# A fused attention and two mixture layers on one core: expert 0's scalings placed later, routing steps reordered, SP in program order

## The chip, the cores and the metric

The kernel runs on one core of a Trainium2 chip. Five engines run side by side, each from its own in-order queue: TensorE (PE, matmuls, with PEld for its weight loads), VectorE (DVE), ScalarE (ACT), GpSimd (POOL) and SyncE (SP, which here issues transfers). SBUF is the on-chip memory; PSUM has 8 banks that matmuls write. The metric is the device time of one execution in microseconds (us); lower is better.

## The reference, cut to what matters

```
x   = attention(q, k, v)         # 2 x 8 heads, 576 tokens, head 64; masks: 4 heads local, 4 strided -> x [1152, 512]
P   = sinkhorn(exp(x @ w_gate))  # 8 rounds over rows and columns, [1152, 8]
x2  = sum over e of P[:, e] * (relu(x @ w1[e]) @ w2[e])            # 8 experts, 512 -> 1024 -> 512, all tokens
nl  = x2 @ wgate2 + log1p(exp(x2 @ wnoise)) * noise
top = two largest of nl per token; w = softmax over the two
out[t] = sum over its two experts e of w * (relu(x2[t] @ v1[e]) @ v2[e])
```

Everything is float32. A matmul of full precision is made of three passes over operands split into a high and a low part (`mm3`).

## The kernel before, in words

Tokens lie in 9 tiles of 128. The first mixture is dense. Expert 0 comes first, in four quarters of its hidden width, summed unscaled into `acc[:, t]`, because P isn't known yet: the Sinkhorn rounds run on DVE meanwhile. Then line 610 multiplies the nine tiles of `acc` by P[:, 0] on ACT, and experts 1 to 6 follow, each in four quarters q. A quarter computes the hidden layer with the seven products p1 to p7 of a Strassen-Winograd scheme, in two halves of the tokens (`Unit`; `keep` on line 643 copies a product out of its bank as `s1` or `s5`, and p6 may write over the bank only then), and then nine `pair2` calls that DVE adds into `acc`, scaled by P (line 561). Weights are fetched by SP into two raw buffers (line 132; 110 in the later stages) and split by ACT and DVE (lines 103 and 105). All this is outside any hand-written order: a planner, which simulates the program with costs of its own, picks for each engine among the instructions that are ready the one that stands earliest in the program, unless it was given a higher priority.

Expert 7 of the first mixture (`g1`: up, `g2`: down, by tiles), the routing of the second mixture, and its expert 0 stand in a block with a hand-written order (`tc.manual_schedule(engines=ORDERED)`, line 893): there the engines named in ORDERED (PE, DVE, ACT) keep the program's order among the block's instructions; POOL and SP are left to the planner, which may also move work from behind the block between them. The list `between` holds steps that `mm3` calls one by one after each matmul, so that small steps are interleaved with large matmuls.

Routing works on three tiles at a time: r0 (tiles 0 to 2), r3 (3 to 5), r6 (6 to 8). `turn(i)` writes a finished tile to the DRAM table `x2d`, transposes it (line 377) and copies it (line 379). `steps` multiplies it by the gate weights (`lp`, line 387; `lg2`, line 396). `choose` finds the two largest (ACT for exp and log, DVE for the rest; the choice is `m`, line 431), `weigh` makes the weights, `place` ranks the tokens of each expert with small matmuls (`rank`, lines 449 to 453) and lets POOL write six blocks of list entries to the DRAM `table` by indirect DMA (line 474). For r6, `sort`, `assemble` and `collect` build the last tokens of expert 0 on chip with one-hot matrices `hot`. `gather` loads a list (SP, line 531) and pulls the rows of its tokens (POOL, line 536); `prep` transposes them (line 722) and splits them.

Expert 0 of the second mixture runs with its up layer (`up`) and its `Down` parts: part (j, h) is token tile j with half h of the hidden width, and POOL adds its result into `out` by indirect DMA (line 795). `rank` orders the other seven experts by load; SP reads their order into registers (line 869), with which the fetches of their weights are addressed. `look` loads their lists. The seven experts follow (`expert`), each with 256 tokens and a rest of 88 to 32 (CAPS - 256); rests up to 64 take `Down.tail`, unsplit matmuls whose output is cut into m pieces across partitions (lines 809 and 813). For the last expert PE keeps program order. A loop behind it, for overfull experts, isn't entered here.

PSUM banks are handed out in turn per tag, two each for a, b, c and d. Routing and `prep` use b; `g1` uses d; `g2` uses a and c.

Of the kernel before, what the change touches and what calls it, by code (L numbers as in the profile page):

```python
# [9 lines left out]
F32 = mybir.dt.float32  # L10
# [4 lines left out]
AF = mybir.ActivationFunctionType  # L15
# [6 lines left out]
NT = N // 128  # L22
# [39 lines left out]
def tile_kernel(ctx: ExitStack, tc: tile.TileContext, qL, kL, vL, qS, kS, vS, wg, u12, w1, w2, wgn, noise, v1, v2, cst, dummy, out):  # L62
# [304 lines left out]
    class Route:  # L367
# [14 lines left out]
        def steps(self):  # L382
            def product(i):
                if i == 0:
                    self.lp = ps("b", "lp")
# [7 lines left out]
            def total(i):  # L393
                if i == 0:
                    self.lg = ps("b", "lg2")
                nc.tensor.matmul(self.lg[:, i * 2 * E:(i + 1) * 2 * E], self.parts[:, i], fold2, start=True, stop=True)
# [212 lines left out]
    for t in range(NT):  # L609
        nc.scalar.activation(acc[:, t], acc[:, t], AF.Copy, scale=P[:, t, 0:1])  # L610

# [67 lines left out]
    for e in range(1, E - 1):  # L679
        for q in range(NP):  # L680
            raw = fetch_u(e, q)
            a, b = conv_wino(raw[0]), conv_u2(raw[1])
            for u in range(2):
# [10 lines left out]
                for_later = [x.p4, x.p3]  # L694
            y = [partial(pair2, b, t, e) for t in (0, 1, 5, 4, 2, 3, 6, 7, 8)]
# [77 lines left out]
    class Down:  # L773
# [28 lines left out]
        def tail(self, raws, hr, tt, k):  # L802
# [9 lines left out]
            for j in range(m):  # L812
                nc.scalar.activation(y[:k, j * d:(j + 1) * d], p[j * w:j * w + k, :d], AF.Copy,
                                     scale=tt[:k, 1:2].bitcast(F32))
# [36 lines left out]
    def rank():  # L851
# [17 lines left out]
        _, values = nc.values_load_multi_w_load_instructions(ordi[:1, :], engines=(mybir.EngineType.SP,), min_val=1, max_val=E - 1)  # L869
        order.extend(values)  # L870
        return past, key, spot
# [20 lines left out]
    ORDERED = {mybir.EngineType.PE, mybir.EngineType.DVE, mybir.EngineType.Activation}  # L892
    with tc.manual_schedule(engines=ORDERED):
# [26 lines left out]
        g2(*b1, (5,), e, False)  # L920
        r0.choose()
        r3.turn(1)
        g1(*a0, whole[2:], 0, (0,))
        r0.weigh()
        r3.turn(2)
        spread(r3, 0, 2, 6, 9, 10, 11)
        r0.place(EARLY, float(LATE))
        g1(*a0, whole[2:], 0, (1,))
# [17 lines left out]
        vs = [conv_w(raws[0])]  # L946
        g2(*b1, (7,), e, False)
        r6.turn(0)
        g2(*b1, (8,), e, False)
        r6.turn(1)  # L950
        prep([x for _, x in got], [128] * len(got), 0)
# [12 lines left out]
        ranked = rank()  # L964
        raws = [fetch_w(weights(v1, order[0], h)) for h in range(2)]
        look()
# [3 lines left out]
        d0 = Down(vs, [t for t, _ in got], [128] * len(got), 0)  # L970
        r6.assemble()
        d0.part(0, 0)
# [5 lines left out]
        rows.product(0)  # L978
        d0.part(1, 1)
        rows.turn(0)  # L980
        rows.product(1)
        ws = [conv_w(raws[0])]
# [6 lines left out]
    def expert(i, ws, got):  # L989
# [19 lines left out]
        d.part(1, 0)  # L1009
        d.tail(raws, tail, tts[2], k)  # L1010
# [105 lines left out]
```

## Time and profile before

| what | value |
|---|---|
| median of 3 runs | 1129.57 us (1128.79 to 1131.33) |
| the profiled execution, its own time | 1126.98 us |
| its span, first to last instruction | 1125.0 us |
| mean granted TensorE clock, share of full | 0.994 |
| PE busy | 1095.7 us, 97% of the span |
| DVE, ACT, POOL busy | 664.7, 393.7, 185.2 us (59%, 35%, 16%) |
| DMA | 98.71 MB, mean 88 GB/s |

Times inside the profile count from the start of the span. Attention and expert 0 of the first mixture fill the first 170 us, experts 1 to 6 go to about 735 us, the hand-ordered block from there to about 900 us, and the seven routed experts to the end. A share of busy time is a mean over these stages; waits are read where they stand.

### The profile page before, as it was taken

The numbers are of one execution on the slowest core, as the hardware profiler recorded it, in microseconds if no ns is written. First come the engines' busy times: TensorE is split into PE (matmuls) and PEld (weight loads), VectorE is DVE, ScalarE is ACT, GpSimd is POOL, SyncE is SP. The second block draws the span as 40 slices with busy tenths as digits, with TensorE's granted clock in tenths as the row PEclk, the third lists the DMA queues.
The fourth block names the chain that finished last, engine by engine and source line by source line (L and its number), as shares of the span: only waits on it lengthen the run. The fifth ranks groups of instructions, "written<-read, shape, count | busy, mean of one in ns | idle before, by whom it ended". The sixth has DMA issues, their size and how long they took to land.

```text
span 1125.0 us, 16986 instructions
## 1 busy us (share of the span) xinstructions
PE 1095.7 (97%) x6683; PEld 959.7 (85%) x6683; DVE 664.7 (59%) x1362; ACT 393.7 (35%) x884; POOL 185.2 (16%) x221
## 2 busy tenths in 40 slices
PE   7999999999999999999999999999998999999996
PEld 6787988999898998899988999899787788888885
DVE  5876795676666766666666666643356364544440
ACT  5631334333322333223332233221133263544441
POOL 3410132111111111211111110000041411222211
PEclk9999999999999999999999999999999999999998
DMA  9711152111111111111111111021122782555541
GB/s 304 217 52 73 38 174 86 38 63 50 38 39 38 55 59 38 38 38 51 64 38 39 38 46 68 4 109 38 57 48 76 175 318 27 195 194 194 171 100 23
DMA packets 31071, 98.71 MB, mean 88 GB/s; under 512 B 6506, under 2 KB 14954, under 8 KB 22412
## 3 DMA queue, kind: packets, MB, share of 16 engines
q1 hardware_dynamic: 16028, 80.52, 20.7%
q0 software_dynamic: 5200, 10.17, 4.5%
q10 hardware_dynamic: 9760, 6.89, 2.0%
q8 instruction: 54, 0.88, 0.3%
q14 instruction: 29, 0.24, 0.1%
HBM read 86.06 MB, written 11.60 MB: 87 GB/s over the span
## 4 chain that ended last, share of the span: by engine, by line
PE 88%; DVE 5%; DMA 3%; ACT 2%; issue 1%; SPq 0%; POOL 0%; POOLq 0%; DVEq 0%; ACTq 0%
PE y L163 42%; PE h L163 16%; PE a L637 13%; PE b L637 7%; PE d L637 3%; PE y L809 2%; DMA raw<-in_u 1%; PE xgt L722 1%; DMA qs<-in_qS 1%; DVE wl L105 1%; DMA wg_sb<-in_wg 1%; DVE u1l L105 1%; DVE acc L565 0%; PE ot L240 0%; ACT acc L610 0%
## 5 line engine op out<-in xcount | busy, mean ns | idle before, releaser
L561 DVE SCALAR_TENSOR_TENSOR acc<-y,P,acc 128x512 f32<-128x512 f32 x216 | 159.4, 748 | 147.0 <-PE y L163 147.0
L163 PE MATMUL y<-u2h,gh 128*128 128x512 f32 x504 | 198.5, 394 | 0.4 <-DVE acc L561 0.4
L163 PE MATMUL y<-u2l,gh 128*128 128x512 f32 x504 | 197.5, 392 | 0.0
L163 PE MATMUL y<-u2h,gl 128*128 128x512 f32 x504 | 189.8, 392 | 0.4 <-DVE gl L101 0.3
L153 POOL TENSOR_TENSOR ut<-raw 128x256 f32<-128x256 f32 x48 | 35.0, 751 | 509.8 <-DVE u1l L105 430.0
L163 PEld LDWEIGHTS y<-u2h,gl 128*128 128x128 f32 x504 | 94.4, 188 | 20.9 <-DVE gl L101 1.7
L163 PE MATMUL h<-xl,wh 128*128 128x384 f32 (+8 forms) x352 | 110.8, 315 | 0.0
L163 PE MATMUL h<-xh,wh 128*128 128x384 f32 (+8 forms) x352 | 109.9, 315 | 0.6 <-ACT xh L103 0.3
L163 PE MATMUL h<-xh,wl 128*128 128x384 f32 (+8 forms) x352 | 110.1, 313 | 0.0
L163 PEld LDWEIGHTS y<-u2h,gh 128*128 128x128 f32 x504 | 94.8, 188 | 15.8 <-issue 0.8
L163 PEld LDWEIGHTS y<-u2l,gh 128*128 128x128 f32 x504 | 94.8, 188 | 14.2
L100 ACT ACTIVATE hh<-h 128x256 fp32r<-128x256 f32 (+2 forms) x88 | 35.8, 415 | 99.8 <-PE h L163 96.0
L163 PEld LDWEIGHTS h<-xh,wh 128*128 128x128 f32 x352 | 66.5, 190 | 2.0 <-DVE hl L101 0.6
L163 PEld LDWEIGHTS h<-xl,wh 128*128 128x128 f32 x352 | 66.6, 189 | 1.5 <-issue 1.0
L103 ACT ACTIVATE u2h<-raw 128x1024 fp32r<-128x1024 f32 x31 | 32.9, 1061 | 98.9 <-PE y L163 98.9
L163 PEld LDWEIGHTS h<-xh,wl 128*128 128x128 f32 x352 | 66.6, 189 | 0.3 <-issue 0.2
L101 DVE SCALAR_TENSOR_TENSOR hl<-h,hh 128x256 fp32r<-128x256 f32 (+2 forms) x88 | 40.5, 464 | 38.8 <-ACT hh L100 37.0
L637 PE MATMUL a<-sh,u1h 128*128 128x288 f32 x192 | 57.4, 299 | 2.7 <-ACT s L643 2.7
L105 DVE TENSOR_TENSOR wl<-raw,wh 128x1024 fp32r<-128x1024 f32 x42 | 49.5, 1221 | 17.6 <-ACT wh L103 17.6
L637 PE MATMUL a<-sh,u1l 128*128 128x288 f32 x192 | 57.3, 298 | 0.0
L637 PE MATMUL a<-sl,u1h 128*128 128x288 f32 x192 | 57.1, 298 | 0.0
L637 PE MATMUL b<-sh,u1h 128*128 128x288 f32 x192 | 56.7, 295 | 0.0
(245 smaller groups left out, 2497.7 us busy)
## 6 DMA issues: line engine op xcount, KB each, us to landing
raw<-in_u SPq DMA_DIRECT2D x31, 1024.0 KB, 4.7
raw<-in_v SPq DMA_DIRECT2D x20, 1024.0 KB, 8.9
acc<-in_v SPq DMA_DIRECT2D x12, 1024.0 KB
raw<-in_w SPq DMA_DIRECT2D x4, 1024.0 KB
out<-zero ACTq DMA_DIRECT2D x1, 3072.0 KB
x2d<-acc ACTq DMA_DIRECT2D x9, 256.0 KB, 2.0
vs<-in_vL SPq DMA_DIRECT2D x4, 432.0 KB, 10.1
acc<-in_qL SPq DMA_DIRECT2D x3, 576.0 KB
```

The source lines that it names most:

```text
L100: seen[0] = nc.scalar.activation(hi, src, AF.Relu)
L101: nc.vector.scalar_tensor_tensor(lo, src, 0.0, hi.bitcast(F32), op0=ALU.max, op1=ALU.subtract)
L103: seen[0] = nc.scalar.activation(hi, src, AF.Copy)
L105: nc.vector.tensor_tensor(lo, src, hi.bitcast(F32), op=ALU.subtract)
L153: nc.gpsimd.tensor_tensor(t[:, o], x, y, op=ALU.subtract)
L163: nc.tensor.matmul(o, a, b, start=start, stop=stop)
L561: nc.vector.scalar_tensor_tensor(acc[:, t], p, P[:, t, scale:scale + 1], acc[:, t], op0=ALU.mult, op1=ALU.add)
L637: nc.tensor.matmul(p, l[:, b, c], m, start=first and i == 0, stop=i == 5, skip_group_check=not first)
L722: nc.tensor.transpose(p[:, o:o + k], xg[:k, c * 128:(c + 1) * 128], ident[:k, :k])
L809: nc.tensor.matmul(p[j * w:j * w + k, :d], hr[:, f, :k], raws[f // 4][:, f % 4, j * d:(j + 1) * d], start=f == 0, stop=f == 7)
```

## The change

Seven edits. (1) The nine scalings of line 610 now stand in the program behind the fourteen products of expert 1's first quarter. (2) `lp` takes a bank of tag a and `lg2` one of tag c. (3) r3's turns 1 and 2 move ahead of r0's choose and weigh; r0's place moves behind the next quarter of g1. (4) SP joins ORDERED. The four steps of expert 0's `prep` are spread over g2's tile 8, one after every third matmul; the conversion of v2's first half moves behind tile 8. (5) `rank` no longer loads the registers; `names` loads one before the fetch of the first expert's v1 and six behind it. (6) Part (0, 0) moves ahead of `assemble`; the conversion of the first ordered v1 half moves ahead of part (1, 1). (7) In the last expert, the tail comes behind all four parts; in every tail, odd pieces are read by DVE.

```diff
@@ -382,7 +382,7 @@
         def steps(self):
             def product(i):
                 if i == 0:
-                    self.lp = ps("b", "lp")
+                    self.lp = ps("a", "lp")
                 for c in range(NC):
                     nc.tensor.matmul(self.lp[32 * c:32 * c + 32, i * 128:(i + 1) * 128], wgn_sb[:, c], self.xt[i][:, c],
                                      start=True, stop=True)
@@ -392,7 +392,7 @@
 
             def total(i):
                 if i == 0:
-                    self.lg = ps("b", "lg2")
+                    self.lg = ps("c", "lg2")
                 nc.tensor.matmul(self.lg[:, i * 2 * E:(i + 1) * 2 * E], self.parts[:, i], fold2, start=True, stop=True)
 
             return [partial(product, i) for i in range(RB)] + [partial(total, i) for i in range(RB)]
@@ -606,9 +606,6 @@
         marks.append(seen[0].ins)
     with tc.issue_after(marks[1]):
         sums()
-    for t in range(NT):
-        nc.scalar.activation(acc[:, t], acc[:, t], AF.Copy, scale=P[:, t, 0:1])
-
     with tc.issue_after(seen[0].ins):
         nc.scalar.dma_start(wgn_sb, wgn)
         nc.scalar.dma_start(noise_sb, noise)
@@ -692,6 +689,9 @@
                 x.p2()
                 x.p7()
                 for_later = [x.p4, x.p3]
+            if e == 1 and q == 0:
+                for t in range(NT):
+                    nc.scalar.activation(acc[:, t], acc[:, t], AF.Copy, scale=P[:, t, 0:1])
             y = [partial(pair2, b, t, e) for t in (0, 1, 5, 4, 2, 3, 6, 7, 8)]
             y[0]()
             x.p4()
@@ -810,8 +810,11 @@
                                      start=f == 0, stop=f == 7)
             y = gpool.tile([128, DM], F32, tag="y", name="y", bufs=3)
             for j in range(m):
-                nc.scalar.activation(y[:k, j * d:(j + 1) * d], p[j * w:j * w + k, :d], AF.Copy,
-                                     scale=tt[:k, 1:2].bitcast(F32))
+                o, r, f = y[:k, j * d:(j + 1) * d], p[j * w:j * w + k, :d], tt[:k, 1:2].bitcast(F32)
+                if j % 2:
+                    nc.vector.tensor_scalar(o, r, f, None, op0=ALU.mult)
+                else:
+                    nc.scalar.activation(o, r, AF.Copy, scale=f)
             self.send(y, tt, k)
 
     def down(ws, tts, ns, o, last=False):
@@ -866,9 +869,11 @@
         nc.vector.tensor_tensor(big, spot, iota8[:, None, 1:].to_broadcast([128, n, n]), op=ALU.mult)
         nc.vector.tensor_reduce(at, big, axis=AX.X, op=ALU.add)
         nc.vector.tensor_copy(ordi, at)
-        _, values = nc.values_load_multi_w_load_instructions(ordi[:1, :], engines=(mybir.EngineType.SP,), min_val=1, max_val=E - 1)
+        return past, key, spot
+
+    def names(i, j):
+        _, values = nc.values_load_multi_w_load_instructions(ordi[:1, i:j], engines=(mybir.EngineType.SP,), min_val=1, max_val=E - 1)
         order.extend(values)
-        return past, key, spot
 
     def limits(past, key, spot):
         n = E - 1
@@ -889,7 +894,7 @@
     bigi = cpool.tile([1, 1], I32, name="bigi")
 
     raws = fetch_w(w1[0, 1]), fetch_w(w2[0, 1])
-    ORDERED = {mybir.EngineType.PE, mybir.EngineType.DVE, mybir.EngineType.Activation}
+    ORDERED = {mybir.EngineType.PE, mybir.EngineType.DVE, mybir.EngineType.Activation, mybir.EngineType.SP}
     with tc.manual_schedule(engines=ORDERED):
         g1(*a0, whole[:2], 0, (0, 1, 2))
         a1 = conv_w(raws[0])
@@ -918,14 +923,14 @@
         g2(*b1, (4,), e, False)
         r3.turn(0)
         g2(*b1, (5,), e, False)
+        r3.turn(1)
         r0.choose()
-        r3.turn(1)
         g1(*a0, whole[2:], 0, (0,))
+        r3.turn(2)
         r0.weigh()
-        r3.turn(2)
         spread(r3, 0, 2, 6, 9, 10, 11)
+        g1(*a0, whole[2:], 0, (1,))
         r0.place(EARLY, float(LATE))
-        g1(*a0, whole[2:], 0, (1,))
         r3.choose()
         g1(*a0, whole[2:], 0, (2, 3))
         r3.weigh()
@@ -943,12 +948,13 @@
         raws = [fetch_w(v2[0, h]) for h in range(2)]
         g1(*a1, whole[2:], 0, (1, 2, 3))
         g2(*b1, (6,), e, False)
-        vs = [conv_w(raws[0])]
         g2(*b1, (7,), e, False)
         r6.turn(0)
+        for step in prep_steps([x for _, x in got], [128] * len(got), 0):
+            between.extend((None, None, step))
         g2(*b1, (8,), e, False)
+        vs = [conv_w(raws[0])]
         r6.turn(1)
-        prep([x for _, x in got], [128] * len(got), 0)
         r6.turn(2)
         spread(r6, 0, 1, 9, 18, 19, 20)
         up(ws, 0, 0, EARLY, (0,), "dac")
@@ -962,24 +968,26 @@
         r6.place(HEAD, over)
         up(ws, 0, 0, EARLY, (6,), "dac")
         ranked = rank()
+        names(0, 1)
         raws = [fetch_w(weights(v1, order[0], h)) for h in range(2)]
+        names(1, E - 1)
         look()
         r6.sort()
         up(ws, 0, 0, EARLY, (7,), "dac")
         got1 = fetch(0)
         d0 = Down(vs, [t for t, _ in got], [128] * len(got), 0)
+        d0.part(0, 0)
         r6.assemble()
-        d0.part(0, 0)
         d0.part(0, 1)
         d0.part(1, 0)
         late = r6.collect(EARLY)
         limits(*ranked)
         rows = Rows(ws, EARLY, EARLY, LATE)
         rows.product(0)
+        ws = [conv_w(raws[0])]
         d0.part(1, 1)
         rows.turn(0)
         rows.product(1)
-        ws = [conv_w(raws[0])]
         got = got1
         prep([x for _, x in got], sizes(0), 384)
         rows.turn(1)
@@ -1007,6 +1015,11 @@
         d = Down(vs, tts[:2], (128, 128), 0)
         d.part(0, 0)
         d.part(1, 0)
+        if last:
+            d.part(0, 1)
+            d.part(1, 1)
+            d.tail(raws, tail, tts[2], k)
+            return ws, got
         d.tail(raws, tail, tts[2], k)
         d.part(0, 1)
         d.part(1, 1)
```

## Rows read from the trace of the kernel before

**Rows 1.** Waits of TensorE, whole run: total us, times, longest us
```profile
PE a L637 <- ACT s L643: 2.7, 1, 2.7
...
PE late L504 <- DVE hot L493: 1.6, 1, 1.6
...
PE xgt L722 <- DVE xl L105: 1.8, 3, 1.3
```

**Rows 2.** Timeline of ACT: start, us, instruction, count, [idle before and its releaser]
```profile
169.18 3.79 ACT L610 ACTIVATE acc<-acc,P 128x512 f32<-128x512 f32 x6 [1.81 <-DVE P L331]
...
173.17 1.04 ACT L103 ACTIVATE u2h<-raw 128x1024 fp32r<-128x1024 f32 x1
...
175.34 0.39 ACT L643 ACTIVATE s<-a 128x288 f32<-128x288 f32 x1
```

**Rows 3.** Windows: stretch, busy us by engine (instructions), TensorE clock, DMA share, GB/s
```profile
176.00:178.00 2.00, 2.00 (x9) 2.00 (x10) 1.42 (x4) 1.34 (x4) 0.00 (x0) 0.50 0.75 197
...
178.00:180.00 2.00, 2.00 (x11) 1.84 (x10) 0.92 (x3) 0.00 (x0) 0.00 (x0) 0.70 0.78 328
...
1120.00:1121.00 1.00, 0.00 (x0) 0.00 (x0) 0.00 (x0) 0.00 (x0) 0.00 (x0) 0.50 0.56 98
```

**Rows 4.** Timeline (first row) and chain of waits (others) at r0's ranking
```profile
810.71 0.60 PE L377 MATMUL x2t<-cs,acc 128*128 128x128 f32 x4
...
814.64 1.58 PE h L163 x4
...
818.78 4.26 PE h L163 x24
```

**Rows 5.** Timeline of DVE in the choices and placings of r0 and r3
```profile
809.05 0.17 DVE L409 TENSOR_SCALAR u<-ez 128x24 f32<-128x24 f32 x1
...
811.75 0.18 DVE L431 TENSOR_TENSOR m<-oh 128x24 bf16<-128x24 f32 x1
...
812.87 0.17 DVE L455 TENSOR_TENSOR rk<-rank,cs 128x24 f32<-128x24 f32 x1
...
814.04 0.17 DVE L471 COPY en<-w 128x6 f32<-128x6 f32 x1
...
822.44 0.18 DVE L431 TENSOR_TENSOR m<-oh 128x24 bf16<-128x24 f32 x1
```

**Rows 6.** Timeline of POOL: r3's first and last scatter, the first pull
```profile
826.25 0.98 POOL L474 DMA_INDIRECT table<-en,si  x1 [2.21 <-DVE en L471]
...
833.29 0.95 POOL L474 DMA_INDIRECT table<-en,si  x1 [0.30 <-issue]
...
842.67 0.99 POOL L536 DMA_INDIRECT xg<-x2d,tt  x1 [8.43 <-DMA tt<-table]
```

**Rows 7.** SP's queue: half of v2, the lists, v1 of expert one
```profile
832.05 0.33 SPq L110 DMA_DIRECT2D raw<-in_v  x1
...
839.53 1.91 SPq L531 DMA_DIRECT2D tt<-table  x2
...
873.31 1.43 SPq L110 DMA_DIRECT2D raw<-in_v  x2
```

**Rows 8.** Chain of waits: tile 8 of g2, first `up`, the second preparation
```profile
846.72 2.79 PE y L163 x12
...
853.39 0.12 PE h L163
...
890.39 2.35 DVE wl L105 x2
...
893.23 0.52 PE xgt L722 x3
```

**Rows 9.** SP's register loads: ns min/median/max, first and last start
```profile
L869 SPq TENSOR_LOAD <-ordi x1: 1142/1142/1142, 868.6 to 868.6; - x1
...
L869 SPq SEQ_ASSERT  x7: 3/18/356, 870.0 to 872.6; - x7
```

**Rows 10.** Timeline of POOL: the last scatter
```profile
1116.44 1.56 POOL L795 DMA_INDIRECT out<-y,tt  x1 [1.24 <-ACT y L791]
```

## The prediction

> **What bounds the kernel now.** I read the busy shares first: TensorE is busy nearly the whole span, so only its idle or slowed time can be won. The list of what TensorE waited for shows where: one wait of 2.7 us for ACT's copy `s` in the first quarter of expert 1, 1.6 us for `hot` before the first down product, 1.8 us for `xl` in the preparations of gathered tokens [rows 1]. Then I read the engines' timelines at these places and summed, by the start-to-start distance of matmuls, where TensorE runs below its usual pitch. The losses lie at 172 to 179, 808 to 823, 849 to 853, 867 to 869 and 889 to 894 us, and after the last matmul. The change touches all six.
>
> The profiled execution took 1126.98 us (span 1125.0), 2.6 us less than the median of the runs, 1129.57. I sum on the former and subtract the result from the latter.
>
> **Scalings of expert 0.** ACT gets P at 169.18 us and then runs six scalings (3.79 us, 0.63 each), a conversion of the next quarter's weights (1.04) and two more scalings before the copy `s<-a` at 175.34, for which TensorE waits [rows 2, 1]. After that wait the granted clock is 0.50, the lower of the two levels, for two microseconds and 0.70 over the next two [rows 3]: 2 x 0.5 + 2 x 0.3 = 1.6 us more are lost. Moved into the text behind the products of that quarter, the scalings rank behind `s<-a`. But this is not in the hand-ordered block: the planner fills an idle ACT with whatever is ready, as it does when it puts a conversion from later text between the scalings [rows 2]. They are ready earlier than `s<-a` in its account, so most stay ahead. Bounds: nothing moves (0, or 0.7 lost if one scaling now holds up an accumulation), everything moves (2.7 + 1.6 = 4.3 gained). I take two of the eight scalings out of the way, 1.2 us, because ACT is otherwise free there. The nine scalings themselves cost nothing as long as ACT idles between the copies.
>
> **Routing steps, tiles 0 to 5.** Now r0's choice stands ahead of r3's second turn, so r0's ranking waits for DVE, `lp` waits for its bank, and the clock falls: four `h` matmuls take 1.58 us where 24 take 4.26 [rows 4]. Afterwards r0.place comes one quarter of g1 later. TensorE then does the second quarter with r3's products inside: 12 x 0.175 + six small steps, about 4.1 us from 811.1 (the third turn's transposes end there but for the wait that follows [rows 4]), to 815.2; r0's ranking follows, and two quarters (4.26 us, rows 4) end at 819.6. DVE is later: the splitting of the second quarter's result ends about 1.0 us behind the matmuls (from the 24 matmuls' start to the end of r3's `m` is 3.8 us, less the choice's 2.9), 816.3; place takes 1.35 us (812.87 to 814.21), choose 2.9 (809.05 to 811.93) [rows 5], so `m` of r3 is there at 820.6 instead of 822.6. TensorE waits about 1 us for it, a new wait, and is still 2.0 us ahead. Bounds: 3.5 (no wait) and 0.3 (the clock falls again, 1.7 us as now). The banks that `lp` and `lg2` take from the rotations `a` and `c` come free within one tile, so I cost this at nothing; a bank kept until the choice has read it could cost a tile's evacuation, 0.8 us.
>
> **First gather, SP in order.** r0's six scatters start 3.5 us later, at 818.0 (0.3 behind the end of place), and r3's cannot pass them: at the pitch of r3's own (826.25 to 834.24, 8.0 us) POOL is free at about 826, and r3's last scatter ends at 834.5, not earlier than now [rows 6]. So the table is no sooner complete while TensorE is 2.0 us ahead. In SP's queue the two small list loads now stand ahead of both halves of v2; today one half goes out at 832.05 and the lists wait until 839.53 for the table [rows 7]. Without that megabyte in flight the table may land up to 2.5 us sooner. The pulls start 3.1 us after the lists, at 842.67 [rows 6], and end some microseconds later. On today's clock I bound the arrival of the gathered tiles by 845.2 (the second pull's issue ends 2.3 us behind the first's start, and all comes 0.3 later) and 850.3 (today's transposes, just before 850, do not wait for data), and take 846.5, as the table should be earlier. They are wanted at 846.7 - 2.0 + 0.7 = 845.4, inside tile 8 of g2: a wait of 1.1 us. The preparation spread over tile 8 shortens the stretch from that tile to expert 0's first `up` (846.72 to 853.39, rows 8) by 0.4 (bounds: 2.0 more, as the transposes' own waits go; 2 less, as r6's copies now queue on ACT behind the conversion of v2's first half, two pieces of 1.0 us, as u2h's [rows 2]). Sum: 0.7 lost of the 2.0.
>
> The Trainium skill (DMA: Bandwidth & Descriptors, Queues, rings and completion order) says that each DMA engine goes round between its queues packet by packet. By that the pulls, on another queue, share with the two megabytes of v2 instead of standing behind them, which is the early half of my bounds; had they to wait for all of it, the late end would hold.
>
> **hot.** Part (0, 0) now runs before the interleaved assembly: 2.8 us of matmuls cover the 1.6 us wait [rows 1]. 1.7 gained with the restart. Next in line is the copy of the late tokens, which has part (1, 0) to hide behind. Bounds 0 and 1.7.
>
> **One register ahead.** SP loads seven numbers from 868.6 to 872.6 and issues v1 of the first ordered expert at 873.31 [rows 9, 7]. The load itself takes 1.14 us, to 869.75, and the seven numbers 2.85; one number takes 0.4, so the issue comes 2.4 us earlier. This pays twice: the conversion can stand ahead of part (1, 1), so the 2.35 us of `wl` no longer lie between TensorE's last row product and the transposes of expert 0's tokens [rows 8]; and its megabytes leave before the last table entries. The six further numbers, loaded afterwards, lie under the wait for the table. From 889.6 to 893.5 TensorE does under 1 us of work, so it loses 3.0 now; I take back 2.0, but the gathered tokens come off the same chain as before (scatters, lists, pulls), are just in time today and would be late by about 0.8 against a TensorE that comes earlier: 1.2 gained. Bounds: 3.0, and -1.7 (the wait returns all of `hot`).
>
> The Trainium skill (Runtime: NRT & Kernel Launch, Instruction fetch mechanics) gives about 200 ns per loaded register, so six fewer would be an estimated 1.2 us; the rows say 0.4 each, assertion included, and I go by them.
>
> **Tail last.** Now the last work is part (1, 1); POOL issues its 128 rows from 1116.44 for 1.56 us [rows 10], and the DMA engines are 0.56 busy up to 1121 [rows 3]. Afterwards the last piece has 32 rows; its four quarters are read by ACT and DVE, two each, and the scatter of 128 rows starts 2 us earlier. Same TensorE work; the end comes 0.3 (POOL's issue alone) to 2.2 us (the data of one large scatter) sooner; I take 1.4, most of a scatter's data. Halves on DVE for experts 1 to 5 run beside TensorE and cost nothing; a DVE queue of conversions ahead of them could hold one bank, 0.5 at most in all.
>
> **Sum.** -1.2 - 2.0 + 0.7 - 1.7 - 1.2 - 1.4 = -6.8; I round it to -6.5 for the small transposing steps, which each break a matmul run for about 0.1 us. 1120.5 for a profiled execution, 1123.1 for the runs.
>
> **Rivals.** (a) The planner clears the copy: 4.3 instead of 1.2 at expert 1, 1120.0. For it: nothing but the scalings fills ACT there; against: the fill-in order seen now. Chance 0.22.
> (b) The gathers bound both starts: arrival at the late end eats the 2.0 of the routing, the second chain eats `hot`, expert 1 gives nothing; the tail alone stays: 1128.2. For it: the pulls are the last link and POOL's scatters aren't earlier. Against: there is less in flight beside them. 0.17.
> (c) SP's order makes it slower. The lists hold SP until the table is complete, as it stood between 832.4 and 839.5 [rows 7], and both halves of v2 go out after them. If the tiles come at 850.3, `up` starts some 5.3 us behind (nine matmuls of tile 8, 2.1; three more steps, r6's two turns and the accumulation between them, an estimate from the 6.7 us of rows 8), at 855.6, 2.2 later than now; the conversion of v2 then stands waiting at the head of ACT's queue with r6's copies behind it (+2), and a TensorE idle that long falls to the lower clock (+1.7). With the tail (-1.4), expert 0's preparation (-2.0), and `hot` returned as a wait and nothing at expert 1, +2.5: 1132.1. It decides from an arrival of about 849 on. 0.11.
> Forecast 0.50.
>
> A measurement of this kernel can tell about 0.2%, 2.3 us. The forecast and (a) lie beyond it on the fast side, (c) on the slow side; (b) is inside, with a few of its variants on either side: faster 0.74, same 0.15, slower 0.11. The forecast's own range is 1120 to 1126; with (a)'s upper gain and part of (b) and (c) the range is 1117.5 to 1130.0.
>
> **What would show it.** TensorE's wait for `s` near 173 us: 2 us left (forecast) or under 0.6 (a). A new wait of `rank` for r3's `m` of about 1 us and no stretch at the lower clock near 815. A wait of `xgt` for `xg` in tile 8 of g2: about 1 us, or over 3 for (b) and (c). No wait for `hot`. v1's issue about 2.4 us behind the load of the order rather than 4.7. DMA work up to 3 us behind POOL's last issue instead of 4.6. I am wrong if expert 1's wait is unchanged and `xgt` waits take over what routing and `hot` give.

## The result and the profile after

The changed kernel is slower: 1139.6 us (median of 19 runs, 1138.12 to 1151.81) against 1131.02 for the kernel before (19 runs beside them, 1127.02 to 1139.75). The ratio on record is 1.0098, with a 95% interval of 1.0073 to 1.0124 (the two medians alone give 1.0076). I had forecast 6.5 us less; it became 8.6 more, and the time lies outside the range.

The profiled execution took 1150.36 us, its span is 1148.2. One thing has to be set aside first: executions differ by some 9 us in the attention part at the start, which the change does not touch (its last `ot` matmul starts at 76.0 to 77.5 us in some profiles of this document and at 81.6 to 87.0 in the others), and this one has the long start. Its first product `a` of expert 1 starts at 180.13 us, that of the profile before at 171.12. So I measure from that product on, between marks that both kernels have: the starts of the first `x2t` transpose (r0's first turn), of r6's `rank` product and of the first `ht` transpose, the end of the last matmul and the end of the span. All are read from TensorE's timeline; differences in us:

| kernel | `a` to `x2t` | to r6's `rank` | to `ht` | to last matmul | to the end | from `a`, all |
|---|---|---|---|---|---|---|
| before | 621.9 | 71.0 | 22.3 | 229.0 | 9.6 | 953.9 |
| changed | 623.1 | 78.2 | 20.5 | 235.8 | 10.5 | 968.1 |
| difference | +1.3 | +7.2 | -1.8 | +6.7 | +0.9 | +14.2 |

The runs differ by less than these two profiles: the profile before is one of the shorter executions of its kernel, and this one, at 1150.36, one of the longer of its own. What TensorE waited for in the changed kernel from 150 us on, longest first (total us, times, longest us; answers to [rows 1]):

```profile
PE cnt L526 <- POOL cnt L462: 7.3, 1, 7.3
PE xgt L722 <- DMA xg<-x2d,tt: 5.8, 3, 4.1
PE a L634 <- ACT s L640: 2.7, 1, 2.7
...
PE rank L449 <- DVE m L431: 0.7, 1, 0.7
```

The first two were not there before. The third is there as before, and the wait for `hot` is gone.

**Expert 1.** ACT's timeline in its first quarter (answers to [rows 2]):

```profile
178.19 1.34 ACT L694 ACTIVATE acc<-acc,P 128x512 f32<-128x512 f32 x2 [1.81 <-DVE P L331]
...
179.73 2.55 ACT L694 ACTIVATE acc<-acc,P 128x512 f32<-128x512 f32 x4
182.18 1.04 ACT L103 ACTIVATE u2h<-raw 128x1024 fp32r<-128x1024 f32 x1
183.13 1.32 ACT L694 ACTIVATE acc<-acc,P 128x512 f32<-128x512 f32 x2
184.35 0.39 ACT L640 ACTIVATE s<-a 128x288 f32<-128x288 f32 x1
```

Eight scalings stand ahead of `s<-a` again. The planner put them there although their text had moved behind the products.

**First routing.** POOL's timeline (answers to [rows 6]), then TensorE's beside it:

```profile
826.33 0.76 POOL L462 TENSOR_TENSOR cnt<-cnt,m 128x8 bf16<-128x8 bf16 x3 [150.74 <-PE rank L453]
828.68 1.17 POOL L474 DMA_INDIRECT table<-en,si  x1 [1.59 <-DVE d L413]
...
835.23 0.96 POOL L474 DMA_INDIRECT table<-en,si  x1 [0.30 <-issue]
836.22 0.21 POOL L462 TENSOR_TENSOR cnt<-cnt,m 128x8 bf16<-128x8 bf16 x1
836.60 0.98 POOL L474 DMA_INDIRECT table<-en,si  x1 [0.17 <-issue]
...
842.94 0.96 POOL L474 DMA_INDIRECT table<-en,si  x1 [0.30 <-issue]
843.93 0.48 POOL L462 TENSOR_TENSOR cnt<-cnt,m 128x8 bf16<-128x8 bf16 x2
```

```profile
836.78 0.40 PE L163 MATMUL y<-wh,hl 128*128 128x512 f32 x1
844.47 0.17 PE L526 MATMUL cnt<-cnt,onesb 128*128 128x8 bf16 x1 [7.29 <-POOL cnt L462]
844.49 0.78 PE L163 MATMUL y<-wh,hh 128*128 128x512 f32 x1
845.06 0.63 PE L163 MATMUL y<-wl,hh 128*128 128x512 f32 x1
```

place() adds the chosen tokens to a count in three small steps on POOL and then issues six scatters there. POOL's order is not written by hand. In the changed kernel the planner laid one of r3's three additions between the two sets of scatters and two behind all of them. `total()`, behind tile 7 of g2's first half, multiplies this count: TensorE stands for 7.29 us and then starts its matmuls 0.43 apart, at the lower clock, as two windows show (columns as in [rows 3]):

```profile
842.00:844.00 2.00, 0.00 (x0) 0.00 (x0) 0.00 (x0) 0.00 (x0) 1.67 (x3) 0.50 0.02 1
...
846.00:848.00 2.00, 2.00 (x6) 1.57 (x5) 1.16 (x2) 0.00 (x0) 0.00 (x0) 0.50 0.06 1
```

**Second gather.** SP's, POOL's and TensorE's timelines (r6's `rank` product starts at 881.48; answers to [rows 7, 8]):

```profile
887.08 0.96 SPq L110 DMA_DIRECT2D raw<-in_v  x2
898.62 4.80 SPq L840 DMA_DIRECT2D tt<-table  x7
904.29 0.34 SPq L110 DMA_DIRECT2D raw<-in_v  x1
...
893.84 1.62 POOL L795 DMA_INDIRECT out<-y,tt  x1 [2.06 <-ACT y L791]
903.16 1.00 POOL L536 DMA_INDIRECT xg<-x2d,tt  x1 [7.69 <-DMA tt<-table]
904.46 0.96 POOL L536 DMA_INDIRECT xg<-x2d,tt  x1 [0.30 <-issue]
...
906.64 0.30 PE L722 MATMUL xgt<-cs,xg 128*128 128x128 f32 x1 [1.29 <-DMA xg<-x2d,tt]
911.05 0.48 PE L722 MATMUL xgt<-cs,xg 128*128 128x128 f32 x1 [4.11 <-DMA xg<-x2d,tt]
```

Two things are new. The first scatter-add of expert 0's rows (`out<-y`) goes out 12.4 us behind the rank product and ahead of the pulls; in the profile before, the pulls came first (from 19.8 us) and it followed at 26.2. And the next fetch of 1 MB (v2 of the first ordered expert) leaves at 904.29, among the pulls; before, it left at 892.77, behind them.

**The end.** The chain that ended last (start, duration, what), answer to [rows 10]:

```profile
1135.84 1.93 PE y L809 x64
...
1137.84 0.37 ACT y L817
...
1138.23 0.35 DVE y L815
...
1138.61 0.37 ACT y L817
...
1139.01 0.36 DVE y L815
```

ACT and DVE write the four pieces of `y` one after the other. From the last matmul's end (1137.77) to the end of the last piece it is 1.6 us; before, one eviction of 0.69 us did it in 0.8. From the start of the last scatter to the end of the span it is 8.6 us in both kernels, though the DMA engines fall idle some 3.5 us behind that start instead of 4.6.

### The profile page after: what moved, and what is told of

The parts are those of the page before. It is cut to its first block, busy times and chain, and to the rows that moved or that the text cites. A ratio compares the mean times of both kernels' runs of the same rounds, so it can differ in the third digit from the quotient of the medians.

```text
span 1148.2 us, 16990 instructions
## 1 busy us (share of the span) xinstructions
PE 1112.0 (97%) x6683; PEld 975.8 (85%) x6683; DVE 668.8 (58%) x1369; ACT 391.6 (34%) x877; POOL 183.4 (16%) x221
## 4 chain that ended last, share of the span: by engine, by line
PE 89%; DVE 4%; DMA 2%; POOL 1%; ACT 1%; issue 1%; SPq 0%; POOLq 0%; ACTq 0%; DVEq 0%
PE y L163 41%; PE h L163 16%; PE a L634 13%; PE b L634 6%; PE d L634 3%; PE y L809 2%; PE sc L218 2%; PE xgt L722 1%; PE ot L240 1%; POOL table L474 1%; PE tr L234 1%; DMA acc<-in_qL 1%; DMA table<-en,si 1%; DVE u1l L105 1%; DVE wl L105 1%
## 5 line engine op out<-in xcount | busy, mean ns | idle before, releaser
L163 PEld LDWEIGHTS y<-u2l,gh 128*128 128x128 f32 x504 | 94.8, 188 | 14.2
```

The costliest lines, as they stand in the source:

```text
L163: nc.tensor.matmul(o, a, b, start=start, stop=stop)
```

## Experiments

Each kernel is the changed one with the edit shown. Ratios are to the kernel before, in runs beside it; where none stands, one execution was profiled. The stages are those of the table above; all rows for TensorE's waits have the same three numbers as above. `tc.issue_after(x)` keeps the instructions of its block behind x in the queue of x's engine.

A stage is read from one profile per kernel, and the same order of instructions does not always take the same time. From `x2t` to `rank`, place_back and best2 have the same order on every engine and take 69.0 and 71.6; cnt_dve and best1 take 72.7 and 70.2. From `ht` to the last matmul, the changed kernel, cnt_dve, place_back and scal_hold have the same order and take 233.8 to 235.8. So a difference of less than about 2.5 us in these two stages shows nothing by itself; a wait that comes or goes in every kernel with the edit does.

**cnt_dve**: the counts on DVE.

```diff
-                nc.gpsimd.tensor_tensor(cnt, cnt, m[:, i], op=ALU.add)
+                nc.vector.tensor_tensor(cnt, cnt, m[:, i], op=ALU.add)
```

> The changed kernel with the three additions to the count of each place() on DVE instead of POOL; the rest as it is. Theory (the addition of r3 stands behind r0's six scatters, and two of its three behind r3's six as well, on POOL): the total's wait for the count of 7.3 us falls under 1, the clock stays at 1.00 so that tile 8 behind it takes 2.8 instead of 5.3 us, and the kernel gets 9 to 10 us shorter (lower cluster 1138.8 to about 1129). Rival 1 (the reordered routing itself is late: r3's chosen mask or ranks): a wait of 5 us or more stays in front of the total, 0 to -2 us. Rival 2 (the first gather binds next, since TensorE reaches the first xgt transpose 10 us earlier, at some 855 us by the trace of after, while the pulls are issued at 848.9 and 850.2): a wait of 2 to 4 us for xg appears there, and 6 to 8 us are gained.

1136.66 us, ratio 1.0045 (1.0007 to 1.0083). The waits:

```profile
PE xgt L722 <- DMA xg<-x2d,tt: 7.4, 5, 4.0
...
PE cnt L526 <- DVE cnt L462: 0.6, 1, 0.6
```

The 7.3 us are gone; in the eight kernels that keep the changed order on POOL the wait is 7.2 to 7.3. `x2t` to r6's `rank` takes 72.7 instead of 78.2, so 5.5 of them are kept here (8.0 in best1). The first gather takes a part back, as rival 2 said: two of the five waits for `xg`, 1.9 us, stand there.

**place_back**: r0.place() where it was.

```diff
+        r0.place(EARLY, float(LATE))
         g1(*a0, whole[2:], 0, (1,))
-        r0.place(EARLY, float(LATE))
```

> The changed kernel with r0.place() put back ahead of the second block of g1 (f = 1), where it stood before the change; the counts stay on POOL and the other reordered steps as they are. Theory (r0.place moved late is what lets the planner lay r3's count additions on POOL among and behind scatters): all three additions of r3 stand ahead of its scatters again, the total's wait falls from 7.3 us to under 1, and from the first x2t transpose to r6's rank product it takes 69 to 71 us instead of 78.2 (71.0 before the change), 7 to 9 us gained in all. Rival 1 (the moved turns of r3 are what costs): the wait stays over 5 us. Rival 2 (without the cover of the late placing TensorE waits for r0's mask or for the gathered rows instead): a new wait of 2 us or more, and less than 6 us gained.

1135.39 us, ratio 1.002 (0.9977 to 1.0063). POOL's order is the old one again, by the moved line alone:

```profile
833.06 0.95 POOL L474 DMA_INDIRECT table<-en,si  x1 [0.30 <-DVE q L432]
834.04 0.76 POOL L462 TENSOR_TENSOR cnt<-cnt,m 128x8 bf16<-128x8 bf16 x3
836.36 0.98 POOL L474 DMA_INDIRECT table<-en,si  x1 [1.55 <-DVE en L471]
```

No wait for the count is left, none for the first gather, and the stage takes 69.0, 2.1 less than before the change. 1.3 of the 2.1 are there by r3's `rank` product (28.57 us behind the first `x2t` instead of 29.88): before, the clock fell in that stretch ([rows 4]), here it did not. But in best2, with the same order, it fell again, that product came after 29.84, and the stage took 71.6. So it is shown that the late r0.place brought the wait for the count; that the reordered turns and the spread preparation gain without it is not.

**pool_order**: only POOL's queue put right, with r0.place() left late.

```diff
-                nc.gpsimd.tensor_tensor(cnt, cnt, m[:, i], op=ALU.add)
+                counted = nc.gpsimd.tensor_tensor(cnt, cnt, m[:, i], op=ALU.add)
...
+                    with tc.issue_after(counted.ins):
+                        st = nc.gpsimd.indirect_dma_start(
...
+        with tc.issue_after(lastpull[0].ins):
+            d0.part(0, 1)
```

> The changed kernel with nothing moved but POOL's queue: the scatters of each place() are kept behind its own count additions, and the first send of d0 behind the three pulls of ordered expert 0; r0.place() and v1's conversion stay where the change put them. Theory (what the change lost over the kernel before is mostly POOL's order, which the planner chooses): the total's wait falls from 7.3 us to under 0.6 and the clock stays at 1.00 behind it; r6's rank product comes 71.5 to 73 us behind the first x2t transpose (78.2 changed, 71.0 before, 72.7 with the counts on DVE, where 1.9 us of waits for the first gather stayed); the first ht to last matmul takes 233 to 234 us as in send_late; 8 to 9 us gained in all, and the kernel stands within 3 us of the kernel before. Rival (the late r0.place itself costs, by its late scatters): a wait of 3 us or more for the total or for the first gather's rows stays, 4 us or less gained.

1144.37 us, ratio 1.0054 (1.0011 to 1.0097); from `a` on 961.4, 6.7 less than the changed kernel.

```profile
PE xgt L725 <- DMA xg<-x2d,tt: 6.5, 3, 3.4
```

The count is no longer waited for, but `x2t` to `rank` still takes 73.5: 3.1 of these 6.5 us now stand at the first gather, and the clock falls behind them (0.50 from 852 to 854). The theory and its rival each hold for a part. In this stage POOL's order costs 4.7 us. A late r0.place costs more on top, 4.5 against place_back's 69.0 and 1.9 against best2's 71.6, since r3's scatters end 42.6 us behind the first `x2t` instead of 39.9 and 41.2.

The lateness does not do this alone. The pulls still go out 47.4 us behind the first `x2t`, earlier than before the change (49.7, [rows 6]). Two other edits meet them. TensorE comes for the rows at 52.5 instead of 56.8, since their preparation is spread over tile 8. And SP, now in program order, sends both halves of v2 just ahead of the pulls, where before one half had gone out ahead of the lists (answers to [rows 7]).

```profile
841.01 0.86 SPq L110 DMA_DIRECT2D raw<-in_v  x2
842.13 1.00 POOL L539 DMA_INDIRECT xg<-x2d,tt  x1 [4.82 <-DMA tt<-table]
849.76 0.30 PE L725 MATMUL xgt<-cs,xg 128*128 128x128 f32 x1 [2.54 <-DMA xg<-x2d,tt]
```

Beside these two megabytes the pulls land 7.2 and 7.5 us after their issue; in the changed kernel, where one megabyte was under way, 3.8. With 3.8 the rows would have been there 51.2 us behind the first `x2t`, 1.3 before TensorE came for them (an estimate from these two profiles). In place_back the pulls take 6.0 and 7.0 beside the same two megabytes, but go out 45.0 us behind the first `x2t`, and nothing waits. So by these figures the wait needs the late scatters and SP's new order together. No run has the late scatters without that order, so this half is an estimate and not shown.

`ht` to the last matmul takes 234.0; that the send gives something there is not shown by this time, as scal_hold takes 233.8 without it.

**conv_late**: the conversion back behind the second row product.

```diff
         rows.product(0)
-        ws = [conv_w(raws[0])]
...
         rows.product(1)
+        ws = [conv_w(raws[0])]
```

> The changed kernel with the conversion of the first raw of ordered expert 0's v1 put back behind rows.product(1), where it stood before the change; the rest as it is. Theory A (the earlier conversion frees the raw buffer, the 1 MB fetch of v2 goes out at 904.3, among the pulls of 903.2 to 908.3, and the pulls land 6 us after their issue): the fetch goes out behind the pulls, a pull lands some 3 to 4 us after its issue, the waits of xgt for xg fall from 5.8 to under 2.5 us, the clock stays at 1.00, and 3 to 5 us are gained. Theory B (the chain of ranks, scatters, table, lists and pulls is itself too late for a TensorE that arrives 4 us earlier than before): the waits stay at 5 us or more and the time within 1 us. Both at half: the waits fall to some 3 us and 2 to 3 us are gained. The conversion behind the second product may then be late for the first h of expert 0: up to 1 us back.

1145.11 us, ratio 1.0098 (1.0057 to 1.0138). `ht` to the last matmul: 232.8 instead of 235.8.

```profile
PE xgt L722 <- DMA xg<-x2d,tt: 3.3, 3, 1.2
```

The fetch of v2 now leaves at 909.47, behind three pulls of 904.10 to 906.65, and the second pull is there 3.6 us after its issue (905.39 to 909.03) instead of 6.6 (904.46 to 911.05). Both theories at half, as priced: 3.0 us gained (1.0 against the fastest kernel with the changed order in this stage), 3.3 us of waits left, where that order has 5.0 to 5.8.

**names_all** and **names_conv**: what keeps the rest late? My next theory blamed v1's early fetch. The split of the names was undone, in the second kernel together with the conversion and the end.

```diff
-        names(0, 1)
+        names(0, E - 1)
         raws = [fetch_w(weights(v1, order[0], h)) for h in range(2)]
-        names(1, E - 1)
```

> The changed kernel with only the split of the names undone: all seven loaded ahead of v1's fetch; the conversion stays early. By the theory of the early v1 fetch the lists go out 0.7 to 1 us sooner behind r6's rank product (16.2 to 16.4 instead of 17.1) and the waits of xgt for xg fall from 5.8 to 4 to 5 us; v1's fetch goes out some 9.3 us behind the rank product instead of 5.6. If the split does not touch the chain of lists, both stay within 0.3 us.

> The changed kernel with three parts undone: all ordered names loaded in one go ahead of v1's fetch, the conversion of v1's first half back behind rows.product(1), and at the end the old order (tail ahead of the second halves, all pieces on ACT). Theory (the fetch of v1's 2 MB, sent 3.6 us earlier behind the first name, shares the DMA engines with r6's scatters and lists, so the table's lists go out 17.1 us behind r6's rank product instead of 16.2 and land 4.5 instead of 3.7 us later; with conv_late this leaves waits of 3.3 us): the lists go out within 16.4 us of the rank product, the waits of xgt for xg fall under 1 us, and from the first ht transpose to the last matmul it takes 229 to 230.5 us (229.0 before, 235.8 changed, 232.8 conv_late); the end behind the last matmul goes back from 10.5 to 9.6 us. Rival (the earlier hot matrices alone bring TensorE 1.85 us sooner to rows that arrive as before): lists as before the change, but 1.5 to 2 us of waits stay and the stretch takes 230.5 to 231.5 us.

The waits of names_all:

```profile
PE xgt L722 <- DMA xg<-x2d,tt: 6.8, 3, 3.7
```

and of names_conv (1144.66 us, ratio 1.006, 1.002 to 1.0101):

```profile
PE xgt L722 <- DMA xg<-x2d,tt: 4.7, 3, 2.0
```

The theory falls. Without the split the lists go out later still (18.1 and 18.8 us behind the rank product; 17.1 in the changed kernel, 17.4 in conv_late, 16.2 before), and the waits are longer. So the split brings the lists forward by 1.0 to 1.4 us. What it gains in time, 0.4 us here (236.1 against 235.8) and 0.6 beside the late conversion (233.4 against 232.8), is too little to be shown by these profiles. In names_conv the old end gives 9.6 again.

**send_late** and **send_conv**: the first send behind the pulls, alone and with the late conversion.

```diff
...
-        nc.gpsimd.indirect_dma_start(out=xg[:n], out_offset=None, in_=x2d[:rows, :],
+        lastpull[0] = nc.gpsimd.indirect_dma_start(out=xg[:n], out_offset=None, in_=x2d[:rows, :],
...
-        d0.part(0, 1)
+        with tc.issue_after(lastpull[0].ins):
+            d0.part(0, 1)
```

> The changed kernel with only this added: the first scatter-add of expert 0's rows to out (send of d0) is kept behind the three pulls of ordered expert 0 on POOL, as it stood before the change, when d0's first half ended later. Theory (the changed kernel issues this send 12.4 us behind r6's rank product, in front of the pulls instead of 26.2 us behind it, and its small writes share the DMA engines with r6's scatters and the lists, with a DMA share of 0.6 to 1.2 at 45 to 70 GB/s from 14 to 20 us behind the product): the lists go out at +16.2 instead of +17.1, the first pull at +19.9 instead of +21.7, and of the 5.8 us of waits of xgt for xg 2 to 4 go; the v2 fetch still falls among the pulls. Rival (the scatters' landing is slowed by v1's 2 MB alone): lists and pulls within 0.3 us of the changed kernel.

> send_late and conv_late together: the send behind the pulls and v1's conversion behind rows.product(1). If the send and the freed buffer are the two causes: lists at +16.2, first pull at +19.9, waits of xgt for xg under 0.5 us in all, clock 1.00 throughout, first ht transpose to last matmul 229 to 230 us (229.0 before, 235.8 changed, 232.8 with conv_late). If the send does nothing: waits of about 3 us, 232.8.

In the changed kernel the DMA engines are busy with 51 packets of 2 KB on POOL's queue from 15.5 to 17.5 us behind the rank product (window: busy us by engine, clock, DMA share, GB/s),

```profile
897.00:899.00 2.00, 2.00 (x10) 1.59 (x10) 0.00 (x0) 0.00 (x0) 0.00 (x0) 1.00 0.70 52
```

and in send_late (15.1 to 17.1 us behind it) they are idle:

```profile
888.00:890.00 2.00, 2.00 (x10) 1.59 (x10) 0.70 (x6) 0.00 (x0) 0.00 (x0) 1.00 0.07 9
```

The lists go out at +15.9 (send_late) and +16.3 (send_conv), as before the change (+16.2), the first pull at +20.4 and +20.3 instead of +21.7. In the six kernels with the early send and the split names the lists go out at +16.9 to +17.6, in the four with the late send at +15.9 to +16.6, so this is the send. `ht` to the last matmul takes 233.6, which is not told apart from the 233.8 to 235.8 without the edit, and with the late conversion 229.7, against 229.0 before: in this profile the two causes together hold 6.1 of the 6.7 us lost there, in best2, which has both edits too, 4.2. Of the waits in send_conv 2.3 us stay, more than the 0.5 expected:

```profile
PE xgt L724 <- DMA xg<-x2d,tt: 2.3, 2, 1.1
```

TensorE reaches the first `ht` 20.5 us behind the rank product, 1.8 earlier than before the change, by what `hot` gave; the rows do not.

**scal_hold**: the scalings really behind `s<-a`.

```diff
-            nc.scalar.activation(s, p, AF.Copy)
+            setattr(self, name + "i", nc.scalar.activation(s, p, AF.Copy))
...
-                for t in range(NT):
-                    nc.scalar.activation(acc[:, t], acc[:, t], AF.Copy, scale=P[:, t, 0:1])
+                with tc.issue_after(x.s1i.ins):
+                    [nc.scalar.activation(acc[:, t], acc[:, t], AF.Copy, scale=P[:, t, 0:1]) for t in range(NT)]
```

> The changed kernel with the nine scalings of expert 0 kept behind the copy s<-a of the second half of expert 1's first quarter, on ACT in a block. Theory (the changed kernel gained nothing there because the planner again put six to eight scalings ahead of s<-a): the wait of 2.7 us of the product a for s vanishes, but eight scalings of 0.64 us now stand ahead of the relu of d, so a new wait of 2 to 4 us for gh comes behind it; the sum from the first a product to the first quarter's end is within 1.5 us of the changed kernel. Forecast's reading (any move behind s<-a is a gain, rival a of the prediction): the wait vanishes, no new one over 1 us comes, and the stretch gets 2.5 us shorter or more.

1142.02 us, ratio 1.0073 (1.0033 to 1.0114). `a` to `x2t` takes 617.8, 5.3 less than in the changed kernel and 4.1 less than before; best1 and best2, which have the edit too, also take 617.8, the ten kernels with the changed order 620.5 to 623.1. ACT's order:

```profile
182.74 0.41 ACT L640 ACTIVATE s<-a 128x288 f32<-128x288 f32 x1 [0.52 <-PE a L634]
183.72 0.41 ACT L640 ACTIVATE s<-a 128x288 f32<-128x288 f32 x1 [0.57 <-PE a L634]
184.03 5.00 ACT L694 ACTIVATE acc<-acc,P 128x512 f32<-128x512 f32 x8
188.93 0.39 ACT L100 ACTIVATE gh<-d 128x288 fp32r<-128x288 f32 x1
```

I had expected the block of 5 us to hold up the relu of `d` and TensorE with it. It holds up the relu; but the planner, with the copies early, gave TensorE other products for that time, no wait of TensorE is listed there, and the clock stays at 1.00 from 182 to 192 us, where it fell to 0.50 in the changed kernel. The prediction's bound of 4.3 was the right size for a true move.

**tail_act**: all pieces on ACT.

```diff
-                if j % 2:
+                if False:
```

> The changed kernel with all pieces of every short tail scaled on ACT (DVE takes none); the order with the tail last stays. Theory (pieces of one y written by ACT and DVE run one behind the other, each with a wait of 0.4 us for the other engine): the four last pieces take 1.45 us in a row on ACT, the last scatter starts 1.4 to 1.6 us behind the last matmul instead of 1.9, 0.2 to 0.5 us gained at the end. Rival (the two engines did overlap and ACT alone is the longer): the last scatter starts 0.3 us or more later than in the changed kernel. Time of the whole within 1 us of the changed kernel by both; the end of the trace decides.

1142.41 us, ratio 1.0085 (1.004 to 1.013). From the last matmul to the end 10.5 us, as in the changed kernel:

```profile
1135.91 1.48 ACT L817 ACTIVATE y<-y,tt 32x128 f32<-32x128 f32 x4 [1.23 <-PE y L809]
...
1137.66 1.35 POOL L795 DMA_INDIRECT out<-y,tt  x1 [1.15 <-ACTq L1034]
```

The hand-over between the engines costs little: four pieces take 1.48 us on ACT and 1.53 on both in turn (1137.84 to 1139.37). What costs is to have four pieces at all behind the last matmul, 0.8 us more than the one eviction of a whole tile, and the smaller scatter does not return it: from its start to the end of the span it is 8.6 us here too.

**best1** and **best2**: the parts that gained, together. best1 is cnt_dve, scal_hold, names_all, the late conversion and the old end; best2 is place_back, scal_hold, send_conv and the old end, with the names split.

> The parts that gained, put together: the changed kernel with the counts on DVE, the scalings kept behind s<-a (scal_hold), all names ahead of the fetch, the late conversion and the old end. If the gains add (scalings -5.3, counts -7.5, names and conversion -5 to -6, end -0.9, all by the distance from the first product a to the end of the span, 968.1 in the changed kernel against 953.9 before): 947 to 950 us there, 4 to 7 us faster than the kernel before the change. If the first gather binds once TensorE comes to it earlier (1.9 us of waits for xg in cnt_dve already): 951 to 954, within 3 us of before.

> All that gained, together: the changed kernel with r0.place() back in its old place, the scalings kept behind s<-a, v1's conversion late, the send behind the pulls, the old end; kept of the change are the reordered turns, the spread first preparation, SP in program order, the split names and the early hot matrices. By stages: A to first x2t 617.8, to r6's rank product 69.0, to the first ht 20.5, to the last matmul 229 to 230.5, end 9.6: 946 to 947.5 against 953.9 before, so 6 to 8 us faster than the kernel before, ratio 0.993 to 0.995. If the send does nothing: 949 to 950, ratio about 0.996.

best1: 1130.67 us, ratio 0.9983 (0.994 to 1.0026), not told apart from the kernel before. best2: 1125.37 us, ratio 0.9929 (0.989 to 0.9968), the one version whose interval lies below 1. From `a` on, where the start does not count, the two take 951.1 and 951.0 against 953.9 before: about 2.9 us gained, less than best2's ratio says; 946 to 947.5 had been expected for best2. In best2 the stage to `rank` takes 71.6 instead of 69.0, with the clock at 0.76, 0.50 and 0.89 in the three windows of 2 us from 810 to 816, and `ht` to the last matmul 231.6, with these waits, at both gathers:

```profile
PE xgt L724 <- DMA xg<-x2d,tt: 3.2, 4, 1.0
```

## Why the prediction was wrong

**Scalings of expert 0**: 1.2 forecast, nothing gained; the lower bound held. The argument was the right one (the planner fills an idle ACT with what is ready), and it should have been followed to its end: whatever keeps two of eight back was never named. The +1.3 of that stage is not shown to be the edit's: nine other kernels with the same order of instructions there took 620.5 to 623.1, and the 621.9 of the kernel before lies among them.

**Routing steps, tiles 0 to 5**: right. r3's `rank` product comes 27.95 us behind the first `x2t` instead of 29.88, 1.9 sooner (2.0 forecast), with 0.7 us of a new wait for `m` (about 1 forecast) and the clock at 1.00 throughout, as forecast.

**First gather, SP in order**: the step that failed first and most. It says that r0's scatters start later, that r3's "cannot pass them", and that POOL is free at about 826. All of this happened. But it counts as waiting behind POOL only the scatters, the table and the pulls. r3's count additions stand in the same queue, and `total()` reads them two tiles of g2 later, long before any gathered row is wanted. I had `total()` in none of my rows. In place of +0.7 the stage lost 9.1 (7.2 net, and 1.9 from the routing): 7.3 of wait and some 2.4 of lower clock behind it (the twelve matmuls behind `total()` take 5.27 us, 849.76 less 844.49; before, the same twelve took 2.88, 828.72 to 831.60); some 0.7 came back between there and r6's `rank`, where the spread preparation stands (31.7 against 32.4). SP's order did for the lists what I had said: they went out 2.3 us behind the end of r3's last scatter instead of 5.3. In the changed kernel it cost nothing, since TensorE stood for the count and no wait for gathered rows followed. With the count out of the way (pool_order) the wait that I priced at 1.1 is 3.1: the rows landed at 847.9 and 848.8 on the clock of the kernel before, within my bounds and behind the 846.5 that I took, beside both halves of v2.

**hot**: right. 1.7 forecast, 1.8 measured.

**One register ahead**: the sign was wrong. v1's issue comes 5.6 us behind the rank product instead of 9.3, of which the split gives 2.2 (7.8 in names_all; 2.4 forecast), and by the lists the split is a gain. The bound of -1.7, rows that are just in time today against an earlier TensorE, was the right thought but too small, because two transfers moved into the gather's way. The earlier conversion frees a buffer, and the fetch that waits for it falls among the pulls. And expert 0's first scatter-add moved ahead of the pulls on POOL. I had asked what lies on the chain, not what the faster steps set free. The stretch lost 6.7 us (4.8 in scal_hold, alike there) where 1.2 were to be gained.

**Tail last**: 1.4 forecast, 0.9 lost. I counted what the smaller scatter saves and not that four small evictions stand where one stood. And the saving isn't there: DMA work does end earlier behind the last issue, as I had forecast, but the span ends 8.6 us behind the start of the last scatter with either size.

Rival (a) was reached only where the scalings were tied (scal_hold, best1, best2), rival (b)'s gathers bound in part, and (c), the one on the slow side, stood at 2.5 us of loss where 8.6 were measured, and named SP's queue where POOL's held the count. What I had named as the sign of being wrong came: the wait for `s` is unchanged at 2.7 us, and waits for gathered rows, 5.8 us, take over what `hot` gave. The largest single wait, for the count, was in neither the sum nor a rival.

## What to carry to other kernels

When a step with DMAs moves, list everything on its queue's engine, small arithmetic too, and ask for each who reads it first; an engine whose order is left to a planner can turn a moved line into a new order far from it. Text moved in a planned region may move nothing, as the scalings here: to hold work back, tie it to the instruction it is to follow. When a conversion gets earlier, look at which transfer waits for its buffer and what that transfer will meet.

## What the runs showed of the hardware

A gather of 128 rows of 2 KB was there 3.5 to 3.6 us after its issue with no fetch beside it (the first two of conv_late), and 6.6 us after it with a fetch of 1 MB issued 0.2 us ahead of it (904.29 and 904.46 in the changed kernel). With two such fetches issued 0.7 to 3.5 us ahead, the first gathers landed after 6.0 to 8.1 us (place_back, pool_order, cnt_dve); with one, issued 1.7 us ahead, after 3.8 (the changed kernel). The Trainium skill (DMA: Bandwidth & Descriptors, Queues, rings and completion order) says that a DMA engine takes turns between its queues packet by packet. The traces agree as far as they go: the gather is slowed by the fetch, and not only when it comes second, since in names_all one issued 1.0 us ahead of the fetch (905.28 and 906.24) still took 6.3 us to land.

A scatter-add of 128 rows is cheap to issue (1.62 us) and dear to others: the DMA engines were 0.70 busy at 52 GB/s in a window in which they otherwise were 0.07 busy, and the lists at the end of a chain of small transfers beside it went out 0.9 us later.

After TensorE's stop of 7.3 us the clock was 0.50 up to 848 us, 0.55 over the next two microseconds of work without a gap, and 1.00 from 850 on. The twelve matmuls behind it took 2.4 us more than before the change, so the stop cost a third more than its own length.
